# Sparse attention feeding a split-precision feed-forward: four heads to an attention piece, with tiles of the TensorE array

## The chip, the cores and the metric

The kernel runs on one core of one Trainium2 chip. A core has five engines that run their own instruction queues in order: TensorE (PE in the profile, with its weight loads as PEld), VectorE (DVE), ScalarE (ACT), GpSimd (POOL) and SyncE (SP), which issues the DMAs here. Semaphores tie them together. The metric is the device time of one execution in microseconds (us). Before the change it is 994.1 us, the median of three runs (993.43 to 994.18).

## The reference

Eight heads of attention over eight sequences of 576 tokens, head size 64, then a feed-forward layer on the 4608 tokens. Heads 0 to 3 are local (a query sees the 32 keys up to itself), heads 4 to 7 are strided (a query sees the earlier keys at the same place modulo 32).

```
scores = scale * np.matmul(q, k.transpose(0, 1, 3, 2))
rel = pos[:, None] - pos[None, :]
mask_local = (rel >= 0) & (rel < stride)
mask_strided = (rel >= 0) & (pos[None, :] % stride == pos[:, None] % stride)
scores = np.where(masks[None, :, :, :], scores, -1000000000.0)
scores = scores - np.max(scores, axis=-1, keepdims=True)
attn = np.exp(scores)
attn = attn / (np.sum(attn, axis=-1, keepdims=True) + 1e-09)
return np.matmul(attn, v).astype(np.float32)
...
x = np.ascontiguousarray(attn_out.transpose(0, 2, 1, 3)).reshape(B * S, H * D)
...
h = x @ w_in
sp = np.maximum(h, 0.0) + np.log1p(np.exp(-np.abs(h)))
g = h * erf(sp)
return (g @ w_out).astype(np.float32)
```

All operands are float32; w_in is 512 x 2048 and w_out 2048 x 512.

## The kernel before

**Feed-forward.** The tokens go in 12 chunks of 384, the 2048 hidden units in 16 tiles of 128, so there are 192 steps. A step (`ftile`) has 12 matmuls into a PSUM tile h (L457; x and w_in are each split into a high and a low part, three products over four row blocks), a chain of ScalarE and VectorE operations (L465 to L498) that ends in ghi and glo, and 9 matmuls into three PSUM tiles o (L527). These are f32r matmuls of one pass.

**Attention pieces.** Each batch has 12 pieces (`piece`, L220): two heads (a pair hp; 0 and 1 local, 2 and 3 strided) and a third j of the sequence. Local pieces take two blocks of 96 queries, strided ones two blocks of 126 queries or, for j = 2, one of 72. The two heads of a pair lie on the two halves of the 128 rows, and the queries are padded with zeros, so that one matmul (L261) over 128 rows gives 128 keys by the queries of both heads: 192, 252 or 144 columns. These are plain f32 matmuls; the trace shows each as two passes, a weight load and a matmul each. The softmax runs along the key partitions: mask (L282, VectorE, from PSUM into sm), maximum over partitions (L287, GpSimd), subtract (L296, VectorE), exponential (L300, ScalarE). Then come the products with v (L304), one for each head and block, with sm as weights (96, 126 or 72 columns) and 65 moving columns, the last of them ones for the sum; the normalisation (L315, L321, L329); a transpose on TensorE (L335); and the split into xhi and xlo (L353, L358), which the h matmuls read.

The first two batches have a form of their own (mask by a matmul); only the batches from the third on are changed.

**What sets the order.** All operations are added to a planner (`Plan`) with a duration, a key (the time when it is due) and the buffers that it opens and uses. `order` then takes, engine by engine, whichever operation can start first, and by key among those that can start together; the program is written out in that order, and on the chip each engine keeps it. The keys of attention pieces spread them over the feed-forward steps of the two batches before. The PSUM ring `ps` has two tiles; scores, av and transposes take one each. SBUF rings: qk 2, v 3, sm 3, mx 2, xn 2, r 2.

Of the kernel before, what the change touches and what calls it, by code (L numbers as in the profile page):

```python
# [8 lines left out]
F32 = mybir.dt.float32  # L9
# [3 lines left out]
AF = mybir.ActivationFunctionType  # L13
ALU = mybir.AluOpType

B, H, S, D = 8, 8, 576, 64
DM, DF = 512, 2048
NT = B * S
P = 128
# [9 lines left out]
PRO, SLOT = 78.281, 5.385  # L29
# [4 lines left out]
A0K, A0S, A0D = 6.648, 4.179, -9.111  # L34
A1K, A1S, A1D = PRO - 0.655, 3.9, 5.799
ASH, ADT = -0.644, 1.759
# [3 lines left out]
QL = 96  # L40
RB = 7
NA = S // 32
QS = RB * NA
WL = 2 * 2 * QL + 2 * QL + 32
WS = 2 * 2 * QS + 2 * P
# [43 lines left out]
class Plan:  # L89
# [13 lines left out]
    def add(self, eng, dur, key, emit, after=(), new=(), use=(), earliest=0.0):  # L103
        op = Op(eng, dur, key, emit, after, new, use, earliest)
        self.ops.append(op)
        return op

    def _ready(self, op, live):
        t = op.earliest
        for p in op.after:  # L110
            if p.end is None:
                return None
            t = max(t, p.end + (self.SAME if p.eng == op.eng else self.LATENCY)[op.eng])
        for b in op.new:
            order = live.setdefault(b.tag, [])
            n = len(order) - self.bufs[b.tag]
            if n >= 0:
                for u in order[n].users:
                    if u.end is None:
                        return None  # L120
                    t = max(t, u.end + (self.SAME if u.eng == op.eng else self.LATENCY)[op.eng])
        return t
# [46 lines left out]
def attention_moe(  # L169
# [10 lines left out]
    nc = tc.nc  # L180
# [3 lines left out]
    apool = ctx.enter_context(tc.tile_pool(name="apool", bufs=2))  # L184
    mpool = ctx.enter_context(tc.tile_pool(name="mpool", bufs=2))
    wpool = ctx.enter_context(tc.tile_pool(name="wpool", bufs=1))
    ps_a = ctx.enter_context(tc.tile_pool(name="ps_a", bufs=2, space=PSUM))
# [3 lines left out]
    xhi = [cpool.tile([P, RING], F32R, name=f"xhi{c}") for c in range(NCC)]  # L191
    xlo = [cpool.tile([P, RING], F32R, name=f"xlo{c}") for c in range(NCC)]
    ident = cpool.tile([P, P], F32, name="ident")
    con = cpool.tile([P, NCON], BF16, name="con")
    mask_l = con[:, : 2 * QL].rearrange("p (b h q) -> p b h q", b=2, h=1)
    mask_s = con[:, 2 * QL : 2 * QL + QS].rearrange("p (u q) -> p u q", u=1)
# [7 lines left out]
    plan = Plan(bufs)  # L204
    pools = {"apool": apool, "mpool": mpool, "wpool": wpool, "ps_a": ps_a, "ps_h": ps_h, "ps_o": ps_o}

    def buf(pool, tag, shape, name, dtype=F32):
        def make():
            return pools[pool].tile(shape, dtype, tag=tag, name=name, bufs=bufs[tag])

        return Buf(tag, make)

    def dve(n, x=1.0):
        return 0.067 + n * x / 960.0

    def act(n, fixed=0.093):
        return fixed + n / 1200.0


    def piece(b, hp, j, key, dt, ring, pe_mask=False, pool_sub=False, early=False):  # L220
# [4 lines left out]
        loc = hp < 2  # L225
        nblk = 1 if (not loc and j == 2) else 2
        n = QL if loc else (QS if j < 2 else S - 4 * QS)
        units, cols = 2 * nblk, 2 * nblk * n
        pid = f"{b}_{hp}_{j}"
        qk = buf("apool", "qk", [P, WS], f"qk_{pid}")  # L230
        v = buf("apool", "v", [P, 2, 2, D + 1], f"v_{pid}")
        s = buf("ps_h", "h", [P, 512], f"s_{pid}") if early else buf("ps_a", "ps", [P, 512], f"s_{pid}")
        sm = buf("apool", "sm", [P, 4 * QS], f"sm_{pid}")
        mx = buf("apool", "mx", [P, 4 * QS], f"mx_{pid}")
        pav = buf("ps_o", f"o{hp % 2}", [P, 512], f"av_{pid}") if early else buf("ps_a", "ps", [P, 512], f"av_{pid}")
        xn = buf("apool", "xn", [P, 4, D], f"xn_{pid}")
        rc = buf("apool", "r", [P, 4, 1], f"r_{pid}")
        pt = buf("ps_a", "ps", [P, 512], f"t_{pid}")
# [121 lines left out]
        add = plan.add  # L360
        w = nblk * n
        lq = add("sp", P * 4 * (WL if loc else nblk * (2 * n + P)) / 3.6e5, key - 8.0, load_qk, new=[qk])
        lv = add("sp", P * 4 * nblk * 2 * (D + 1) / 3.6e5, key - 7.9, load_v, new=[v])
        per = max(2 * n / 600.0, 0.213) + (2 * n / 2400.0 if pe_mask else 0.0)
        o_s = add("pe", 0.02 + nblk * per, key, scores, [lq, *o_con], [s, sm], [qk])
# [11 lines left out]
        o_e = add("act", act(cols), key + dt + 0.1, exp, [o_b], [], [sm, s] if early else [sm])  # L377
        o_v = add("pe", 0.00174*n * units, key + dt + 0.2, av, [o_e, lv], [pav, xn], [sm, v])
        o_r = add("dve", 0.07, key + 1.5 * dt, total, [o_v], [rc], [pav])
        o_r = add("dve", 0.1, key + 1.5 * dt, invert, [o_r], [], [rc])  # L380
        if early:
            o_n = add("act", 0.2 * units, key + 1.5 * dt + 0.1, norm, [o_r], [], [pav, xn, rc])
        else:
            o_n = add("dve", dve(units * D), key + 1.5 * dt + 0.1, norm, [o_r], [], [pav, xn, rc])
        o_t = add("pe", 0.11 * nblk, key + 2 * dt, transp, [o_n] + ring, [pt], [xn])
        o_h = add("act", act(w, 0.06), key + 2 * dt + 0.1, split_hi, [o_t], [], [pt])
        return [add("dve", dve(w), key + 2 * dt + 0.2, split_lo_x, [o_h], [], [pt])]


    def weight(i, src, rows, sl, key):  # L390
# [175 lines left out]
    o = plan.add("sp", 0.6, -20.0, load_consts, new=[con_f])  # L566
    o_con = [plan.add("dve", 0.6, -19.0, copy_consts, [o], [], [con_f])]
# [3 lines left out]
    x_of = {}  # L571
# [3 lines left out]
    for f in range(0, DF, SW):  # L575
        for c in range(NCC):
            i = len(w1)
            rows, sl = slice(c * P, (c + 1) * P), slice(f, f + SW)
            op, pair = weight(i, w_in, rows, sl, W1K[i // 4] + W1S[i // 4] * (i % 4))
            w1.append(op)  # L580
            win.append(pair)
    for f in range(NFC):
        rows, sl = slice(f * P, (f + 1) * P), slice(0, DM)
        op, pair = weight(NFC + f, w_out, rows, sl, W2K + W2S * f)
# [3 lines left out]
    def order(b):  # L588
        if b % 2:
            return [(hp, j) for j in range(3) for hp in (0, 2, 1, 3)]  # L590
        if b == 0:
            return [(0, 0), (1, 0), (0, 1), (1, 1), (2, 0), (3, 0), (2, 1), (3, 1), (2, 2), (3, 2), (0, 2), (1, 2)]
        return [(hp, j) for j in range(2) for hp in range(2)] + [
            (2, 0), (3, 0), (0, 2), (2, 1), (3, 1), (1, 2), (2, 2), (3, 2)
        ]

    def chunk(c):
        need = [o for b in (2 * (c // 3), 2 * (c // 3) + 1) for o in x_of.get((b, c % 3), [])]
        for f in range(NFC):
            k = c * NFC + f  # L600
            ready = (need + w1[4 * (f // 4) : 4 * (f // 4) + 4], [w2[f]])
            mm1_of[k], _ = ftile(k, ready)
            mm1_first.append(mm1_of[k])

    for b in range(B):
        p2 = b // 2
        for i, (hp, j) in enumerate(order(b)):

            if b % 2 == 0:
                to = [0] if (hp < 2 and j < 2) else ([1] if hp < 2 else [0, 1])  # L610
            else:
                to = [1] if (hp < 2 and j == 0) else ([2] if hp < 2 else [1, 2])
            if b == 0:
                key, dt = A0K + A0S * i, A0D
            elif b == 1:
                key, dt = A1K + A1S * i, A1D
            else:
                if b % 2:
                    slot = 48 * p2 - 3 + (15 * i) / 11
                elif i < 4:  # L620
                    slot = 48 * (p2 - 1) + 13 + 4 * i
                else:
                    slot = 48 * (p2 - 1) + 29 + (15 * (i - 4)) / 7
                key, dt = PRO + SLOT * (slot + ASH), ADT * SLOT
            ring = []
            if p2:
                ring = [mm1_of[48 * (p2 - 1) + 16 * c + 15] for c in to]
            done = piece(b, hp, j, key, dt, ring, pe_mask=b < 2, pool_sub=False, early=b == 0)
            for c in to:
                x_of.setdefault((b, c), []).extend(done)  # L630
        if b % 2 == 0:
            continue
        for c in range(3 * p2, 3 * p2 + 3):
            chunk(c)
# [109 lines left out]
```

## Time and profile before

| what | us |
| --- | --- |
| median of three runs | 994.1 |
| profiled execution, its own time | 993.13 |
| its span, first to last instruction | 991.2 |
| third batch's attention to the last piece, about | 118 to 816 |
| score products L261, whole span: union of busy time, 192 / 252 / 144 columns | 43.1 / 33.6 / 6.7 |
| products with v L304, whole span: 96 / 126 / 72 columns | 39.3 / 32.0 / 6.6 |

The union counts a matmul from its start to its modelled end, and neighbours overlap, so these times are longer than what a group takes from the engine. The chain of work that ended last gives that: at each step it goes back to what released an instruction, or to the instruction before it on its engine, and the pieces of the chain add up to the span.

### The profile page before, as it was taken

The numbers are of one execution on the slowest core, as the hardware profiler recorded it, in microseconds if no ns is written. First come the engines' busy times: TensorE is split into PE (matmuls) and PEld (weight loads), VectorE is DVE, ScalarE is ACT, GpSimd is POOL, SyncE is SP. The second block draws the span as 40 slices with busy tenths as digits, with TensorE's granted clock in tenths as the row PEclk, the third lists the DMA queues.
The fourth block names the chain that finished last, engine by engine and source line by source line (L and its number), as shares of the span: only waits on it lengthen the run. The fifth ranks groups of instructions, "written<-read, shape, count | busy, mean of one in ns | idle before, by whom it ended". The sixth has DMA issues, their size and how long they took to land.

```text
span 991.2 us, 15250 instructions
## 1 busy us (share of the span) xinstructions
PE 979.5 (99%) x5443; PEld 885.6 (89%) x5443; DVE 728.7 (74%) x1619; ACT 654.7 (66%) x1481; POOL 152.8 (15%) x100
## 2 busy tenths in 40 slices
PE   8999999999999999999999999999999999999998
PEld 6788999999899989999899999999899999999997
DVE  6999997677677776676777776776767776665664
ACT  4676777567566666666765665766766576766765
POOL 3534111111112110011112110111111210000000
PEclk9999999999999999999999999999999999999999
DMA  9994211111222211111222220211112220000000
GB/s 310 308 338 144 63 35 59 40 40 53 71 62 82 62 37 38 46 53 27 80 58 73 71 63 19 70 40 40 49 53 66 63 63 1 32 2 0 32 1 33
DMA packets 37659, 68.76 MB, mean 69 GB/s; under 512 B 4176, under 2 KB 18640, under 8 KB 37584
## 3 DMA queue, kind: packets, MB, share of 16 engines
q1 hardware_dynamic: 37584, 67.80, 22.1%
q8 instruction: 43, 0.70, 0.3%
q14 instruction: 32, 0.26, 0.1%
HBM read 58.34 MB, written 9.44 MB: 68 GB/s over the span
## 4 chain that ended last, share of the span: by engine, by line
PE 91%; DVE 8%; ACT 0%; issue 0%; DMA 0%
PE h L457 39%; PE o L527 39%; PE s L261 5%; PE av L304 5%; DVE w L415 1%; PE t L335 1%; DVE w L421 1%; DVE pair L429 1%; DVE a L462 1%; DVE w L408 1%; DVE glo L498 1%; DVE b L492 0%; DVE xlo L358 0%; DVE b L462 0%; PE warm L638 0%
## 5 line engine op out<-in xcount | busy, mean ns | idle before, releaser
L527 PE MATMUL o<-pair,ghi 128*128 128x512 f32 x1152 | 372.3, 404 | 0.0
L457 PE MATMUL h<-xhi,pair 128*128 128x384 f32 x1536 | 306.7, 341 | 1.4 <-DVE b L492 1.4
L457 PEld LDWEIGHTS h<-xhi,pair 128*128 128x128 f32 x1536 | 271.9, 188 | 15.7 <-DVE b L492 3.8
L465 ACT ACTIVATE b<-b 128x384 f32<-128x384 f32 x384 | 199.7, 521 | 104.2 <-DVE b L462 101.6
L287 POOL PARTITION_ALL_REDUCE mx<-sm x96 | 152.6, 1594 | 664.1 <-DVE sm L282 568.7
L527 PEld LDWEIGHTS o<-pair,ghi 128*128 128x128 f32 x1152 | 207.0, 188 | 28.0
L527 PE MATMUL o<-pair,glo 128*128 128x512 f32 x576 | 225.9, 392 | 0.0
L457 PE MATMUL h<-xlo,pair 128*128 128x384 f32 x768 | 165.9, 337 | 0.0
L498 DVE TENSOR_TENSOR glo<-b,ghi 128x384 fp32r<-128x384 f32 x192 | 110.5, 576 | 60.3 <-ACT ghi L495 59.8
L462 DVE SCALAR_TENSOR_TENSOR a<-h,a 128x384 f32<-128x384 f32 x192 | 106.4, 554 | 64.9 <-ACT a L465 63.3
L457 PEld LDWEIGHTS h<-xlo,pair 128*128 128x128 f32 x768 | 137.2, 187 | 0.0
L462 DVE SCALAR_TENSOR_TENSOR a<-a,h 128x384 f32<-128x384 f32 x192 | 105.5, 549 | 40.7 <-ACT b L465 38.6
L465 ACT ACTIVATE b<-a 128x384 f32<-128x384 f32 x192 | 100.5, 524 | 47.6 <-DVE glo L498 47.1
L527 PEld LDWEIGHTS o<-pair,glo 128*128 128x128 f32 x576 | 108.1, 188 | 24.1
L495 ACT CAST ghi<-b 128x384 fp32r<-128x384 f32 x192 | 97.9, 510 | 46.8 <-PE o L527 41.6
L492 DVE TENSOR_TENSOR b<-b,h 128x384 f32<-128x384 f32 x192 | 105.1, 547 | 31.2 <-ACT b L465 30.9
L465 ACT ACTIVATE a<-a 128x384 f32<-128x384 f32 x192 | 100.2, 522 | 26.6 <-DVE a L462 24.3
L465 ACT ACTIVATE a<-h 128x384 f32<-128x384 f32 x192 | 92.7, 483 | 33.4 <-PE h L457 32.3
L462 DVE SCALAR_TENSOR_TENSOR b<-b,a 128x384 f32<-128x384 f32 x192 | 110.5, 576 | 3.2
L304 PEld LDWEIGHTS av<-v,sm 128*96 128x96 f32 (+2 forms) x704 | 78.0, 171 | 7.8 <-ACT sm L300 1.5
L261 PE MATMUL s<-qk 128*128 128x192 f32 (+2 forms) x352 | 83.4, 351 | 0.1
L304 PE MATMUL av<-v,sm 128*96 128x65 f32 (+2 forms) x704 | 77.9, 251 | 1.1 <-ACT sm L279 0.7
(34 smaller groups left out, 588.4 us busy)
## 6 DMA issues: line engine op xcount, KB each, us to landing
qk<-qk_loc SPq DMA_DIRECT2D x48, 304.0 KB, 2.8
qk<-qk_str SPq DMA_DIRECT2D x32, 380.0 KB, 3.2
v<-v_all SPq DMA_DIRECT2D x80, 130.0 KB, 2.1
out<-ob SPq DMA_DIRECT2D x36, 256.0 KB, 2.1
words<-w_in SPq DMA_DIRECT2D x16, 512.0 KB, 5.6
words<-w_out SPq DMA_DIRECT2D x16, 512.0 KB, 5.9
qk<-qk_str SPq DMA_DIRECT2D x16, 136.0 KB, 2.1
v<-v_all SPq DMA_DIRECT2D x16, 65.0 KB, 1.9
```

Source lines behind the costliest of these rows:

```text
L261: yield nc.tensor.matmul(dst, qk[:, k0 + blk * step : k0 + blk * step + P], qk[:, blk * 2 * n : (blk + 1) * 2 * n], start=blk == 0, stop=n ...
L287: yield nc.gpsimd.partition_all_reduce(mx[:, :cols], sm[:, :cols], P, ReduceOp.max)
L304: yield nc.tensor.matmul(pav[:n, u * (D + 1) : (u + 1) * (D + 1)], sm[:, u * n : (u + 1) * n], v[:, u // 2, u % 2, :], start=True, stop=True,)
L335: yield nc.tensor.transpose(pt[:, blk * n : (blk + 1) * n], xn[:n, 2 * blk : 2 * blk + 2, :].rearrange("p h d -> p (h d)"), ident[:n, :n],)
L408: yield nc.vector.tensor_scalar(out=w.tile.bitcast(U32), in0=words[:, :, 1], scalar1=0x07FFFFFF, scalar2=3, op0=ALU.bitwise_and, op1=ALU.l ...
L457: yield nc.tensor.matmul(ph[:, :CH], win[4 * s + cc][:, w, fs], x[cc][:, c0 : c0 + CH], start=(i == 0), stop=(i == len(terms) - 1))
L462: yield nc.vector.scalar_tensor_tensor(out=out, in0=in0, scalar=scalar, in1=in1, op0=op0, op1=op1)
L465: yield nc.scalar.activation(dst, src, func, bias=bias[i], scale=scale)
L492: yield nc.vector.tensor_tensor(out=bb.tile, in0=bb.tile, in1=ph[:, :CH], op=ALU.mult)
L495: yield nc.scalar.copy(ghi.tile, bb.tile)
L498: yield nc.vector.tensor_tensor(out=glo.tile, in0=bb.tile, in1=ghi.tile.bitcast(F32), op=ALU.subtract)
L527: yield nc.tensor.matmul(po.tile, g[:, ts], wout[f][:, w], start=(f == 0 and i == 0), stop=(f == NFC - 1 and i == 2),)
```

## The change

From the third batch on, two pairs of heads that are of one kind (0 and 1, or 2 and 3) make one piece, `quad`, in place of two. A batch has 6 of them in place of 12. The parts:

- Scores: for two-block quads, 8 matmuls (L452 of the new kernel), each on the 64 rows of one head, 128 keys by 96 or 126 queries, in one go. The two heads of a pair write different PSUM banks, in turn. The zero padding is no longer read. The short strided quads keep matmuls over 128 rows.
- Mask, maximum, subtract and exponential run once for each bank, that is twice for a two-block quad and once for a short one.
- Products with v: 16 matmuls (L499), each former one parted at query 64, into partitions 0 to 63 and from 64 on, which are two column tiles of the array.
- Normalisation twice, transposes of both pairs into one PSUM tile, split twice.
- The keys: the even batches' quads are 8 and 4 steps apart, the odd batches' 3. The planner's check for free buffers now counts buffers of one ring that one operation opens together. Ring sizes stay.

```diff
-        for b in op.new:
+        for i, b in enumerate(op.new):
             order = live.setdefault(b.tag, [])
-            n = len(order) - self.bufs[b.tag]
+            n = len(order) - self.bufs[b.tag] + sum(x.tag == b.tag for x in op.new[:i])
...
+    def quad(b, loc, j, key, dt, ring):
...
+        hps = (0, 1) if loc else (2, 3)
+        nblk = 1 if (not loc and j == 2) else 2
+        n = QL if loc else (QS if j < 2 else S - 4 * QS)
+        units, w = 2 * nblk, nblk * n
+        tiled = nblk == 2
+        nbank = 2 if nblk == 2 else 1
+        cols = 4 * w // nbank
...
+        s = [buf("ps_a", "ps", [P, 512], f"s{i}_{pid}") for i in range(nbank)]
+        pav = [buf("ps_a", "ps", [P, 512], f"av{i}_{pid}") for i in range(2)]
...
+        def place(i, blk, h):
+
+            if tiled:
+                return h, (2 * i + blk) * n
...
+        def scores():
+            k0, step = units * n, n if loc else P
+            used = set()
+            for i in range(2):
+                for blk in range(nblk):
+                    keys = slice(k0 + blk * step, k0 + blk * step + P)
+                    for h in range(2) if tiled else (slice(0, 2),):
+                        rows = slice(h * D, (h + 1) * D) if tiled else slice(0, P)
+                        bank, c = place(i, blk, h if tiled else 0)
+                        q0 = (blk * 2 + (h if tiled else 0)) * n
+                        width = n if tiled else 2 * n
+                        yield nc.tensor.matmul(
+                            s[bank][:, c : c + width], qk[i][rows, keys], qk[i][rows, q0 : q0 + width],
+                            start=bank not in used,
+                            stop=True, skip_group_check=True,
+                        )
+                        used.add(bank)
...
+        def av():
+            for i in range(2):
+                for u in range(units):
+                    bank, c = place(i, u // 2, u % 2)
+                    for lo, hi in ((0, 64), (64, n)) if tiled else ((0, n),):
+                        yield nc.tensor.matmul(
+                            pav[i][lo:hi, u * (D + 1) : (u + 1) * (D + 1)],
+                            sm[bank][:, c + lo : c + hi],
+                            v[i][:, u // 2, u % 2, :],
+                            start=True,
+                            stop=True,
+                        )
...
+        for k in range(nbank):
+            o = add("dve", dve(cols), key + 0.1 + 0.01 * k, mask(k), [o_s], [], [s[k], sm[k]])
+            o = add("pool", 0.4 + cols * 0.0028, key + 0.2 + 0.01 * k, maxi(k), [o], [mx[k]], [sm[k]], earliest=6.7)
+            o = add("dve", dve(cols), key + dt + 0.01 * k, sub(k), [o], [], [mx[k], sm[k]])
+            o_e.append(add("act", act(cols), key + dt + 0.1 + 0.01 * k, exp(k), [o], [], [sm[k]]))
...
+            for i, (loc, j) in enumerate(pairs(b)):
+                to = chunks_of(b, loc, j)
+                slot = 48 * p2 - 3 + 3 * i if b % 2 else 48 * (p2 - 1) + (13 + 8 * i if i < 2 else 29 + 4 * (i - 2))
```

**Where the instructions move.** All places are the seventh batch, j = 1, local heads. In the names, s is a score tile, av a product with v, t a transpose; a former piece is named by its pair and j (0_1 and 1_1), a quad by batch, kind and j (6_0_1), and the last number only tells buffers apart. The first place is TensorE's row of scores. Before, pair 0 and, some 70 rows later, pair 1 in the same way:

```order
L335 MATMUL t_1_0_6835<-ident,xn_1_0_6763 128x96 x2
L261 MATMUL s_0_1_6840<-qk_0_1_6511 128x192 x2
L527 MATMUL o_6_6178<-pair_1786,ghi_6738 128x512 x2
L527 MATMUL o_6_6178<-pair_1786,glo_6754 128x512
L527 MATMUL o_6_6189<-pair_1786,ghi_6738 128x512 x2
```

Now, both pairs:

```order
L648 MATMUL h_7046<-xlo_83,pair_289 128x384
L452 MATMUL s_6_0_1_7066<-qk_6_0_1_6706 128x96
L452 MATMUL s_6_0_1_7067<-qk_6_0_1_6706 128x96
L452 MATMUL s_6_0_1_7066<-qk_6_0_1_6706 128x96
L452 MATMUL s_6_0_1_7067<-qk_6_0_1_6706 128x96
L452 MATMUL s_6_0_1_7066<-qk_6_0_1_6723 128x96
L452 MATMUL s_6_0_1_7067<-qk_6_0_1_6723 128x96
L452 MATMUL s_6_0_1_7066<-qk_6_0_1_6723 128x96
L452 MATMUL s_6_0_1_7067<-qk_6_0_1_6723 128x96
L718 MATMUL o_6_6336<-pair_1802,ghi_6955 128x512 x2
```

Four matmuls of 192 columns in two places have become eight of 96 in one, in turn into two PSUM tiles. The second place is TensorE's products with v. Before, pair 0 alone:

```order
L457 MATMUL h_6918<-xlo_82,pair_517 128x384
L457 MATMUL h_6918<-xlo_83,pair_483 128x384
L304 MATMUL av_0_1_6941<-v_0_1_6532,sm_0_1_6841 96x65 x4
L457 MATMUL h_6950<-xhi_76,pair_590 128x384
L457 MATMUL h_6950<-xhi_77,pair_558 128x384
```

Now the first eight of sixteen (the other eight, with av_6_0_1_7147, follow at once):

```order
L718 MATMUL o_6_6336<-pair_1940,glo_7062 128x512
L499 MATMUL av_6_0_1_7146<-v_6_0_1_6759,sm_6_0_1_7068 64x65
L499 MATMUL av_6_0_1_7146<-v_6_0_1_6759,sm_6_0_1_7068 32x65
L499 MATMUL av_6_0_1_7146<-v_6_0_1_6759,sm_6_0_1_7069 64x65
L499 MATMUL av_6_0_1_7146<-v_6_0_1_6759,sm_6_0_1_7069 32x65
L499 MATMUL av_6_0_1_7146<-v_6_0_1_6759,sm_6_0_1_7068 64x65
L499 MATMUL av_6_0_1_7146<-v_6_0_1_6759,sm_6_0_1_7068 32x65
L499 MATMUL av_6_0_1_7146<-v_6_0_1_6759,sm_6_0_1_7069 64x65
L499 MATMUL av_6_0_1_7146<-v_6_0_1_6759,sm_6_0_1_7069 32x65
```

Each matmul of 96 queries has become two, of 64 and of 32, and the burst reads both halves of the softmax (7068 and 7069). The third place is VectorE's softmax rows. Before:

```order
L282 TENSOR_TENSOR sm_0_1_6841<-s_0_1_6840,con 128x384
L462 SCALAR_TENSOR_TENSOR a_6858<-h_6799,a_6858 128x384
L492 TENSOR_TENSOR b_6832<-b_6832,h_6741 128x384
L462 SCALAR_TENSOR_TENSOR a_6812<-a_6812,h_6780 128x384
L462 SCALAR_TENSOR_TENSOR b_6866<-b_6866,a_6812 128x384
L498 TENSOR_TENSOR glo_6892<-b_6832,ghi_6876 128x384
L296 TENSOR_TENSOR sm_0_1_6841<-sm_0_1_6841,mx_0_1_6869 128x384
```

Now:

```order
L468 TENSOR_TENSOR sm_6_0_1_7068<-s_6_0_1_7066,con 128x384
L468 TENSOR_TENSOR sm_6_0_1_7069<-s_6_0_1_7067,con 128x384
L653 SCALAR_TENSOR_TENSOR a_7087<-h_7046,a_7087 128x384
L683 TENSOR_TENSOR b_7064<-b_7064,h_6989 128x384
L689 TENSOR_TENSOR glo_7124<-b_7009,ghi_7107 128x384
L483 TENSOR_TENSOR sm_6_0_1_7068<-sm_6_0_1_7068,mx_6_0_1_7097 128x384
L483 TENSOR_TENSOR sm_6_0_1_7069<-sm_6_0_1_7069,mx_6_0_1_7109 128x384
```

Masks and subtracts stand two in a row, with three feed-forward operations between them in place of five. Between the quad's scores and its products with v, TensorE has 12 h and 21 o matmuls.

More of the change, by code (lines that the diff above doesn't have):

```diff
@@ L211, in buf, with named @@
         return Buf(tag, make)
+    def named(name, f):
+        f.__name__ = name
+        return f
     def dve(n, x=1.0):
@@ L387, in piece, with load_qk, load, load_v @@
         return [add("dve", dve(w), key + 2 * dt + 0.2, split_lo_x, [o_h], [], [pt])]
+    def quad(b, loc, j, key, dt, ring):
[6 more added lines that the diff above has]
+        cols = 4 * w // nbank
+        pid = f"{b}_{hps[0]}_{j}"
+        qk = [buf("apool", "qk", [P, WS], f"qk{i}_{pid}") for i in range(2)]
+        v = [buf("apool", "v", [P, 2, 2, D + 1], f"v{i}_{pid}") for i in range(2)]
+        s = [buf("ps_a", "ps", [P, 512], f"s{i}_{pid}") for i in range(nbank)]
+        sm = [buf("apool", "sm", [P, 4 * QS], f"sm{i}_{pid}") for i in range(nbank)]
+        mx = [buf("apool", "mx", [P, 4 * QS], f"mx{i}_{pid}") for i in range(nbank)]
+        pav = [buf("ps_a", "ps", [P, 512], f"av{i}_{pid}") for i in range(2)]
+        xn = [buf("apool", "xn", [P, 4, D], f"xn{i}_{pid}") for i in range(2)]
+        rc = [buf("apool", "r", [P, 4, 1], f"r{i}_{pid}") for i in range(2)]
+        pt = buf("ps_a", "ps", [P, 512], f"t_{pid}")
+        def place(i, blk, h):
+            if tiled:
+                return h, (2 * i + blk) * n
+            c = (blk * 2 + h) * n
+            return (i, c) if nbank == 2 else (0, i * 2 * w + c)
+        def load_qk(i):
+            def load():
+                if loc:
+                    yield nc.sync.dma_start(qk[i][:, :WL], qk_loc[b, hps[i], j])
+                else:
+                    cw = nblk * (2 * n + P)
+                    yield nc.sync.dma_start(qk[i][:, :cw], qk_str[b, hps[i] - 2, j, :, :cw])
+            return load
+        def load_v(i):
+            def load():
+                cw = nblk * 2 * (D + 1)
+                yield nc.sync.dma_start(
+                    v[i].tile.rearrange("p b h d -> p (b h d)")[:, :cw], v_all[b, hps[i], j, :, :cw]
+                )
+            return load
+        def scores():
[15 more added lines that the diff above has]
+                        used.add(bank)
+        def mask(k):
+            def run():
+                src, dst = s[k][:, :cols], sm[k][:, :cols]
+                if loc:
+                    m = (mask_l if j == 0 else mask_l[:, 1:2]).rearrange("p b h q -> p h b q")
+                    r, z, m = "p (i b q) -> p i b q", dict(i=2, b=2), m.broadcast_to([P, 2, 2, n])
+                else:
+                    r, z = "p (u q) -> p u q", dict(u=cols // n)
+                    m = mask_s[:, :, :n].broadcast_to([P, cols // n, n])
+                yield nc.vector.tensor_tensor(
+                    out=dst.rearrange(r, **z), in0=src.rearrange(r, **z), in1=m, op=ALU.add
+                )
+            return named("mask", run)
+        def maxi(k):
+            def run():
+                yield nc.gpsimd.partition_all_reduce(mx[k][:, :cols], sm[k][:, :cols], P, ReduceOp.max)
+            return named("maxi", run)
+        def sub(k):
+            def run():
+                d = sm[k][:, :cols]
+                yield nc.vector.tensor_tensor(out=d, in0=d, in1=mx[k][:, :cols], op=ALU.subtract)
+            return named("sub", run)
+        def exp(k):
+            def run():
+                d = sm[k][:, :cols]
+                yield nc.scalar.activation(d, d, AF.Exp, scale=1.0 / D**0.5)
+            return named("exp", run)
+        def av():
[9 more added lines that the diff above has]
+                            stop=True,
+                        )
+        def norm(i):
+            a, rr = lambda: pav[i][:n, : units * (D + 1)].rearrange("p (u d) -> p u d", u=units), lambda: rc[i][:n, :units]
+            def total():
+                yield nc.vector.tensor_scalar(
+                    out=rr(), in0=a()[:, :, D : D + 1], scalar1=1e-9, scalar2=None, op0=ALU.add
+                )
+            def invert():
+                yield nc.vector.reciprocal(rr(), rr())
+            def scale():
+                yield nc.vector.tensor_tensor(
+                    out=xn[i][:n, :units], in0=a()[:, :, :D], in1=rr().broadcast_to([n, units, D]), op=ALU.mult
+                )
+            return total, invert, scale
+        def transp():
+            for i in range(2):
+                for blk in range(nblk):
+                    c = i * w + blk * n
+                    yield nc.tensor.transpose(
+                        pt[:, c : c + n], xn[i][:n, 2 * blk : 2 * blk + 2, :].rearrange("p h d -> p (h d)"), ident[:n, :n]
+                    )
+        def views(i, t):
+            base, src = (b % 2) * S, pt[:, i * w : (i + 1) * w]
+            if loc:
+                c0 = base + j * 2 * QL
+                return src, t[:, c0 : c0 + w]
+            r0 = 2 * RB * j
+            dst = t[:, base : base + S].rearrange("p (a r) -> p a r", r=32)[:, :, r0 : r0 + w // NA]
+            return src.rearrange("p (r a) -> p a r", a=NA), dst
+        def split(i):
+            def split_hi():
+                src, hi = views(i, xhi[hps[i]])
+                yield nc.scalar.copy(hi, src)
+            def split_lo_x():
+                src, hi = views(i, xhi[hps[i]].bitcast(F32))
+                _, lo = views(i, xlo[hps[i]])
+                yield nc.vector.tensor_tensor(out=lo, in0=src, in1=hi, op=ALU.subtract)
+            return split_hi, split_lo_x
+        add = plan.add
+        lq = [add("sp", P * 4 * (WL if loc else nblk * (2 * n + P)) / 3.6e5, key - 8.0 + 0.1 * i, load_qk(i), new=[qk[i]]) for i in range(2)]
+        lv = [add("sp", P * 4 * nblk * 2 * (D + 1) / 3.6e5, key - 7.8 + 0.1 * i, load_v(i), new=[v[i]]) for i in range(2)]
+        d_s = 1.27 if tiled else 2 * nblk * max(2 * n / 600.0, 0.213)
+        o_s = add("pe", d_s, key, scores, [*lq, *o_con], [*s, *sm], [*qk])
+        o_e = []
+        for k in range(nbank):
[3 more added lines that the diff above has]
+            o_e.append(add("act", act(cols), key + dt + 0.1 + 0.01 * k, exp(k), [o], [], [sm[k]]))
+        o_v = add("pe", 1.23 if tiled else 0.00174 * n * 2 * units + 0.05, key + dt + 0.2, av, [*o_e, *lv], [*pav, *xn], [*sm, *v])
+        o_n = []
+        for i in range(2):
+            total, invert, scale = norm(i)
+            o = add("dve", 0.07, key + 1.5 * dt, total, [o_v], [rc[i]], [pav[i]])
+            o = add("dve", 0.1, key + 1.5 * dt, invert, [o], [], [rc[i]])
+            o_n.append(add("dve", dve(units * D), key + 1.5 * dt + 0.1, scale, [o], [], [pav[i], rc[i], xn[i]]))
+        o_t = add("pe", 0.09 + 0.11 * 2 * nblk, key + 2 * dt, transp, o_n + ring, [pt], [*xn])
+        done = []
+        for i in range(2):
+            hi, lo = split(i)
+            o = add("act", act(w, 0.06), key + 2 * dt + 0.1, hi, [o_t], [], [pt])
+            done.append(add("dve", dve(w), key + 2 * dt + 0.2, lo, [o], [], [pt]))
+        return done
@@ L603, in chunk, with pairs, chunks_of @@
             mm1_first.append(mm1_of[k])
+    def pairs(b):
+        if b % 2:
+            return [(True, 0), (False, 0), (True, 1), (False, 1), (True, 2), (False, 2)]
+        return [(True, 0), (True, 1), (False, 0), (True, 2), (False, 1), (False, 2)]
+    def chunks_of(b, loc, j):
+        if b % 2 == 0:
+            return [0] if (loc and j < 2) else ([1] if loc else [0, 1])
+        return [1] if (loc and j == 0) else ([2] if loc else [1, 2])
     for b in range(B):
         p2 = b // 2
[L607 to L626, printed above, removed]
+        if p2 == 0:
+            for i, (hp, j) in enumerate(order(b)):
+                to = chunks_of(b, hp < 2, j)
+                key, dt = (A0K + A0S * i, A0D) if b == 0 else (A1K + A1S * i, A1D)
+                done = piece(b, hp, j, key, dt, [], pe_mask=True, pool_sub=False, early=b == 0)
+                for c in to:
+                    x_of.setdefault((b, c), []).extend(done)
+        else:
+            for i, (loc, j) in enumerate(pairs(b)):
+                to = chunks_of(b, loc, j)
+                slot = 48 * p2 - 3 + 3 * i if b % 2 else 48 * (p2 - 1) + (13 + 8 * i if i < 2 else 29 + 4 * (i - 2))
                 ring = [mm1_of[48 * (p2 - 1) + 16 * c + 15] for c in to]
-            done = piece(b, hp, j, key, dt, ring, pe_mask=b < 2, pool_sub=False, early=b == 0)
-            for c in to:
-                x_of.setdefault((b, c), []).extend(done)
+                done = quad(b, loc, j, PRO + SLOT * (slot + ASH), ADT * SLOT, ring)
+                for c in to:
+                    x_of.setdefault((b, c), []).extend(done)
         if b % 2 == 0:
```

## The prediction

> **What bounds the kernel now.** I read the share of each engine first, then the chain of work that ended last, then the waits of TensorE in the stretch the change touches. That stretch runs from about 118 us, where the attention of the third batch begins, to 816 us, where the last attention piece is done.
>
> ```profile
> span 991.2 us, 15250 instructions
> PE 979.5 (99%) x5443; PEld 885.6 (89%) x5443; DVE 728.7 (74%) x1619; ACT 654.7 (66%) x1481; POOL 152.8 (15%) x100
> PE 91%; DVE 8%; ACT 0%; issue 0%; DMA 0%
> 118.00:816.00 698.00, 697.33 (x3866) 636.80 (x3865) 512.75 (x1153) 459.49 (x1024) 105.23 (x71) 1.00 0.19 54
> PEld h L457 <- DVE b L492: 2.8, 6, 0.7
> by line: PE h L457 42.0%; PE o L527 40.6%; PE av L304 6.5%; PE s L261 6.5%; PE t L335 1.7%; DVE glo L498 0.7%; DVE a L462 0.6%; DVE b L492 0.4%; DVE sm L282 0.4%; ACT b L465 0.2%; DVE b L462 0.2%; DVE xn L329 0.1%; DVE r L321 0.1%; issue 0.
> ```
>
> The fourth row is the stretch: its length, then the busy time of PE, PEld, DVE, ACT and POOL. PE is busy 697.33 of 698.00 us at a granted clock of 1.00, and the only wait of its weight loads that the stretch shows is 2.8 us. VectorE is busy 512.75 us (73%), ScalarE 66%. So here a microsecond less on TensorE is a microsecond less in the time, as long as no new wait takes its place. The last row is the chain within the stretch: score products (s) and products with v (av) take 6.5% each, 45 us each of 698. This is all the change can win on.
>
> **What one piece costs.** The chain also gives the time by which each group of matmuls pushes PE on, which is what I need; the mean durations of single matmuls overlap and would count twice. From the chain in order of time (start, length, what):
>
> ```profile
> 398.41 2.05 PE o L527 x9
> 400.46 0.17 PE t L335 x2
> 400.62 0.68 PE s L261 x4
> ...
> 406.85 2.12 PE h L457 x12
> ...
> 450.31 0.22 PE t L335 x2
> 450.53 0.65 PE av L304 x8
> ...
> 452.63 0.85 PE s L261 x4
> ...
> 459.22 0.83 PE av L304 x8
> ...
> 473.90 0.65 PE s L261 x4
> ...
> 483.12 0.65 PE av L304 x8
> 483.77 2.18 PE h L457 x12
> 485.95 0.24 PE s L261 x2
> ...
> 492.62 0.25 PE av L304 x4
> L304 PE MATMUL av<-v,sm x516: 217/248/273, 132.1 to 812.7; 128*96 128x65 f32 x93, 128*126 128x65 f32 x64, 128*72 128x65 f32 x15
> L261 PEld LDWEIGHTS s<-qk 128*128 128x128 f32 x352 | 60.7, 193 | 9.0 <-issue 1.9 <-DMA qk<-qk_loc 0.6
> ```
>
> Scores: 0.65 us for a local piece (two f32 matmuls, each in two passes, so four entries, 192 columns moving), 0.85 us for a strided one (252 moving), 0.24 us for a short one (144). Per pass that is 0.162, 0.212 and 0.12 us: 0.84 ns for each moving column. Products with v: 0.65 us in eight passes at 96 weight columns, 0.83 us at 126, 0.25 us in four at 72. Per pass 0.081, 0.104 and 0.062 us, which follows the weight columns at 0.84 ns each, though only 65 columns move (those alone would take 0.055). So a pass costs 0.84 ns times the larger of its weight columns and its moving columns. Behind a product with v the next twelve h matmuls take 2.18 in place of 2.12 us, so I add 0.06 us to each: 0.71 and 0.89.
>
> Batches three to eight have 6 x 6 = 36 local pieces, 24 long strided ones and 12 short ones. The change takes the first 60 pairwise into 30 tiled bursts. Before, these cost 36 x 0.65 + 24 x 0.85 = 43.8 us for scores and 36 x 0.71 + 24 x 0.89 = 46.9 us for av, 90.7 us together. The short ones keep their matmuls (two pieces side by side, no tiles) and the transposes are as many as before; I count both as unchanged. Their 0.24, 0.25 and 0.22 us only stand closer together.
>
> **What a tiled burst costs.** No instruction of before uses part of the array, so I bound it. A score burst is 8 matmuls on 64 rows, 16 passes, each with 128 weight columns and 96 or 126 moving: by the rule above 128 x 0.84 = 0.108 us a pass, whichever piece it is. If the two row halves work side by side, 8 x 0.108 = 0.86 us; if one after the other, 1.73. An av burst is 16 matmuls, 32 passes, with at most 64 weight columns and 65 moving, 0.055 us a pass: 16 x 0.055 = 0.88 us side by side, 1.76 in turn. I take side by side for both, since the halves share neither rows nor PSUM bank in the scores, and neither columns nor partitions in av.
>
> Then there is the change of shape, once into and once out of each burst. It lies between nothing and a full drain with a bare weight load behind it. A 65-column matmul ends no sooner than 217 ns after it starts, 55 of which are its stream, so a drain is some 0.16 us; a 128-column weight load takes 193 ns (last row). I take 0.19 us, the load beginning while the array drains, between the ends 0 and 0.35. It is the value nearest to a row, the 193 ns. So a score burst is 0.86 + 0.38 = 1.24, an av burst 0.88 + 0.38 = 1.26: 1.25 us each, 60 x 1.25 = 75.0 us. Gain: 90.7 - 75.0 = **15.7 us**.
>
> Here a page of the Trainium skill bears on the sum. "TensorEngine Tiling (Array Packing)", section Key Properties, says that changing the tiling mode drains TensorE, not merely changing the tile. No row of before shows it; by it the end at 0 (956 us, the first rival) falls away, and the 979 us below stay.
>
> **New waits.** The av burst now waits for both halves of the softmax. I follow the local quad of the seventh batch whose order stands in the part on the change: between its scores and its av stand 21 o matmuls and 12 h matmuls.
>
> ```profile
> 638.03 0.84 PE L261 MATMUL s<-qk 128*128 128x192 f32 x4
> 640.57 0.55 DVE L282 TENSOR_TENSOR sm<-s,con 128x384 f32<-128x384 f32 x1
> 641.28 1.58 POOL L287 PARTITION_ALL_REDUCE mx<-sm  x1 [18.10 <-DVE sm L282]
> 644.30 0.55 DVE L296 TENSOR_TENSOR sm<-sm,mx 128x384 f32<-128x384 f32 x1
> 644.89 0.53 ACT L300 ACTIVATE sm<-sm 128x384 f32<-128x384 f32 x1
> 647.06 0.81 PE L304 MATMUL av<-v,sm 128*96 128x65 f32 x8
> PE h L457 <- DVE b L492: 0.7, 3, 0.2
> ```
>
> At 2.12 us for twelve h and 2.05 / 9 = 0.228 us for an o, PE has 2.12 + 21 x 0.228 = 6.9 us of other work there. The chain: mask 0.55, 0.16 to POOL (641.28 - 641.12), two reductions of 1.58 one behind the other, subtract 0.55, exponential 0.53: 5.0 us, the second mask lying under the first reduction. That leaves 1.9 us for queueing on VectorE and ScalarE. The piece in the rows lost 1.7 us ahead of its mask (its scores end at 638.87) and 1.4 us ahead of its subtract (641.28 + 1.58 = 642.86), and had 1.6 us to spare before av. In the quad the second kind of loss lies mostly under the second reduction: the new order has three MoE operations, 3 x 0.55 us, between masks and subtracts, some 2.8 us with the masks, while the reductions end after 3.9. The first kind fits in the 1.9 us, just. So most bursts find their input ready and some do not: I take 1.5 us over all 36, say six stalls of a quarter microsecond; the ends are 0 and 36 x 0.4 = 14 us. Behind a stalled av in PE's queue stand o and h matmuls, so a stall is lost in full; so far h waits 0.7 us in the stretch (last row). VectorE and ScalarE keep their work (two masks in a row in place of two apart), so the 73% becomes 75% of a shorter stretch.
>
> A quad takes both qk buffers, so the loads of the next quad go out only after its scores. The two score bursts nearest to each other (the last ones of the fourth batch) have 24 h and 3 o matmuls between them, 2 x 2.12 + 3 x 0.228 = 4.9 us; a load takes 2.1 to 3.2 us to land. I cost it at nothing; without that cover PE would wait some 3 us for each of 36 bursts, and it would be plain as a wait for DMA.
>
> ```profile
> qk<-qk_loc SPq DMA_DIRECT2D x48, 304.0 KB, 2.8
> qk<-qk_str SPq DMA_DIRECT2D x32, 380.0 KB, 3.2
> qk<-qk_str SPq DMA_DIRECT2D x16, 136.0 KB, 2.1
> ```
>
> Sum: -15.7 + 1.5 = -14.2 us. The profiled execution took 993.1 us, 1.9 above its span of 991.2 and 1 below the median of 994.1: 993.1 - 14.2 = **979 us**.
>
> **The rivals.**
> - *Cheap changes of shape.* At 0 instead of 0.38 us a burst: 60 x 0.38 = 22.8 us less, 956 us. For it: weight loads lie beside matmuls nearly always (PEld 89% beside PE 99%), so a load may be hidden across a change too. Against it: a drain of 0.16 us would have to be hidden as well. 0.10.
> - *Dear changes of shape.* At 0.35 each, 0.70 a burst: 60 x 0.32 = 19 us more, 998 us, slower than before. It decides from 0.31 us a change on. 0.07.
> - *The column tiles of av take turns* (slower). Weight loads of one tile can't lie under the other's matmul, so 32 passes come one by one: 0.88 us more in 30 bursts, 26 us, 1005 us. It turns the sign once more than half of the overlap is lost (14.2 / 30 = 0.47 us). For it: both tiles use the same 128 rows. Against it: in the rows below eight weight loads of av lie beside its eight matmuls, on the same rows. 0.12.
>
> ```profile
> 409.26 0.90 PEld L304 LDWEIGHTS av<-v,sm 128*96 128x96 f32 x8
> 409.49 0.81 PE L304 MATMUL av<-v,sm 128*96 128x65 f32 x8
> ```
>
>   The Trainium skill has a rule that gives this outcome: "TensorE: Matmul & The Clock Gate", Part 3 (Packing small matmuls), says that a weight load overlaps running matmuls only where the row group differs. By the two rows that does not hold for the whole array; for column tiles no run here shows it.
> - *The row tiles take turns,* or the parts are no tiles at all, so that the change doesn't do what it says: 0.87 us more in 30 bursts, 26 us, 1005 us; with the one before, 1031 us. 0.06.
> - *The softmax of two pieces comes late:* 14 us of stalls, 979 + 12.5 = 991 us, no change to a little faster. For it: the second reduction. Against: the spare above. 0.08.
>
> **How the numbers follow.** The forecast has 0.57; its own range is 970 to 987 us. The range for 8 in 10 runs from the cheap changes to the dear ones, 956 to 999 us, and leaves out tiles that take turns (0.18). About 2 us (0.2%) is what a measurement of this kernel can tell from no change. Faster: 0.57 + 0.10 + half of the late softmax = 0.71. Same: the rest of it and a part of the dear changes, 0.07. Slower: 0.22.
>
> **What would show it.** In the chain, a burst of 16 score passes and one of 32 av passes should each take about 1.25 us, alike for local and strided quads; s and av should fall from 45 us each in the stretch to about 40. If av bursts take over 2 us, the column tiles take turns; if only the first passes behind a burst stretch, it is the changes. Idle time of PE ahead of av, released by ScalarE's exponential, would be the late softmax. The forecast is wrong if PE stays at 99% and the time does not fall, for then a tiled pass costs more than its columns.

## The result, and the profile after

The changed kernel takes 1027.9 us (median of four runs, 1027.6 to 1028.93) against 994.1 us before: a ratio of 1.0338, 95% interval 1.032 to 1.0356. It is slower by 3.4%, where 979 us and at most 999 had been forecast. The profiled execution has a span of 1025.8 us, 34.6 more than before.

The rows that answer to those of before, from the page, the waits of PE's weight loads and the chain in the stretch from 118 to 850 us (the last attention piece now ends near 850):

```profile
span 1025.8 us, 16728 instructions
PE 1013.7 (99%) x6163; PEld 883.2 (86%) x6163; DVE 722.8 (70%) x1607; ACT 654.1 (64%) x1475; POOL 147.6 (14%) x94
PEld h L648 <- DVE b L683: 1.0, 4, 0.3
PEld av L499 <- ACT sm L490: 0.7, 2, 0.4
by line: PE h L648 41.4%; PE o L718 40.6%; PE av L499 11.8%; PE s L452 4.7%; PE t L529 1.6%
```

PE is still busy 99% of the time, and the h matmuls wait less than before (1.0 us against 2.8). The products with v waited 0.7 us in all for the exponential. So no new wait took the place of the gain: it is PE's own bursts that take longer. The chain says which. Scores fell from 6.5% of 698 us, 45 us, to 4.7% of 732, 34 us. Products with v rose from 45 us to 11.8%, 86 us.

The chain in order of time shows that the rise is in the local bursts alone, 18 of the 30:

```profile
562.03 3.92 PE av L499 x32
568.90 1.09 PE s L452 x16
...
743.61 1.08 PE av L499 x31
744.69 2.28 PE h L648 x12
...
767.59 1.07 PE s L452 x16
768.66 2.28 PE h L648 x12
770.94 4.80 PE o L718 x21
775.73 3.92 PE av L499 x32
```

Score bursts take 1.07 us local and 1.09 strided. Products with v take 1.08 us in a strided quad (one record of 32 is missing at 743.61) and 3.92 in a local one, for the same 32 passes. The chain puts the end of a burst on the group behind it (2.28 us for twelve h in place of 2.12). Measured from the start of the last matmul ahead of a burst to the start of the second one behind it, less two ordinary steps from matmul to matmul (0.176 us after an h, 0.227 after an o), the means are 1.27 and 1.29 us for scores, 1.28 for strided and **4.12 for local products with v**. The forecast had 1.25 for all of them.

One difference between the two kinds is the width of the second column tile: 126 queries are parted into 64 and 62, 96 queries into 64 and 32. The weight loads, each shape apart (busy, mean ns, then idle time of the queue just before them), over the same stretch:

```profile
L499 PEld LDWEIGHTS av<-v,sm 128*64 128x64 f32 x480 | 39.6, 135 | 21.0 <-issue 3.8 <-ACT b L656 3.0 <-ACT ghi L686 1.1
L499 PEld LDWEIGHTS av<-v,sm 128*32 128x32 f32 x288 | 19.8, 108 | 9.8
L499 PEld LDWEIGHTS av<-v,sm 128*62 128x62 f32 x192 | 11.9, 135 | 0.0
```

Ahead of the loads of 62 columns there is no idle time at all. Ahead of those of 32 there are 9.8 us, with no releaser named: the profile shows nothing that was waited for in these pauses. Ahead of those of 64, which open every burst and also follow each tile of 32, there are 21.0 us.

### The profile page after: what moved, and what is told of

It reads as the page before. It is cut to its first block, busy times and chain, and to the rows that moved or that the text cites. A ratio compares the mean times of both kernels' runs of the same rounds, so it can differ in the third digit from the quotient of the medians.

```text
span 1025.8 us, 16728 instructions
## 1 busy us (share of the span) xinstructions
PE 1013.7 (99%) x6163; PEld 883.2 (86%) x6163; DVE 722.8 (70%) x1607; ACT 654.1 (64%) x1475; POOL 147.6 (14%) x94
## 4 chain that ended last, share of the span: by engine, by line
PE 92%; DVE 6%; DMA 1%; issue 0%; ACT 0%; SPq 0%
PE o L718 39%; PE h L648 39%; PE av L499 8%; PE s L452 3%; DVE w L606 1%; DVE w L612 1%; PE t L529 1%; DVE pair L620 1%; DVE w L599 1%; PE s L265 1%; DMA words<-w_in 1%; PE av L308 0%; DVE xlo L362 0%; DMA qk<-qk_loc 0%; DVE a L653 0%; DVE b L653 0%
## 5 line engine op out<-in xcount | busy, mean ns | idle before, releaser
L718 PE MATMUL o<-pair,ghi 128*128 128x512 f32 x1152 | 364.3, 397 | 0.0
L476 POOL PARTITION_ALL_REDUCE mx<-sm x66 | 101.5, 1577 | 641.9 <-DVE sm L468 641.9
L499 PEld LDWEIGHTS av<-v,sm 128*64 128x64 f32 (+2 forms) x1008 | 63.4, 128 | 31.3 <-issue 3.8
L499 PE MATMUL av<-v,sm 128*64 128x65 f32 (+2 forms) x1008 | 89.6, 233 | 0.0
L291 POOL PARTITION_ALL_REDUCE mx<-sm x24 | 45.9, 1929 | 63.9 <-ACT sm L283 58.2
```

The costliest lines, as they stand in the source:

```text
L291: yield nc.gpsimd.partition_all_reduce(mx[:, :cols], sm[:, :cols], P, ReduceOp.max)
L476: yield nc.gpsimd.partition_all_reduce(mx[k][:, :cols], sm[k][:, :cols], P, ReduceOp.max)
L499: yield nc.tensor.matmul(pav[i][lo:hi, u * (D + 1) : (u + 1) * (D + 1)], sm[bank][:, c + lo : c + hi], v[i][:, u // 2, u % 2, :], start=Tr ...
L718: yield nc.tensor.matmul(po.tile, g[:, ts], wout[f][:, w], start=(f == 0 and i == 0), stop=(f == NFC - 1 and i == 2),)
```

## The experiments

The theory that these rows suggest: a tile of 32 columns is another shape of the array than a tile of 64, so each step between them drains the array (a pass of the new shape has to wait until those under way are through). A local burst steps 15 times inside, a strided one never. If 32 passes of 0.055 us come in turn and the way in and out costs 0.38, then 15 x = 4.12 - 1.76 - 0.38 and a step costs 0.13 us. The rivals: that tiles cost as much in any widths, that local pieces are slow for another reason, and that a tile of 32 is slow in itself. All kernels keep the planner's durations and keys of the changed kernel.

**Local products with v whole.**

```diff
-                    for lo, hi in ((0, 64), (64, n)) if tiled else ((0, n),):
+                    for lo, hi in ((0, 64), (64, n)) if tiled and not loc else ((0, n),):
```

> The products with v of the local quads go back to whole matmuls of 96 weight columns, the strided ones keep their two column tiles of 64 and 62. In the profile of the changed kernel a strided av burst took 1.28 us and a local one (tiles of 64 and 32) 4.12 us. Theory 1 (a column tile of 32 after one of 64 is another shape of the array, and each change of shape drains it, 0.13 us each, 15 times inside a local burst): a local burst becomes 16 passes of 0.085 us, 1.4 us, 18 bursts save 18 x 2.7 = 49 us, 979 us, 1.5% faster than before. Theory 2 (tiled av costs whatever its widths, and the strided bursts only look cheap because their cost is recorded elsewhere): the saving is less than half of that, the time stays above 1003 us.

It took 978.8 us, ratio to before 0.9851 (0.9828 to 0.9874). All of the loss, and a gain of 1.5%, hang on the local products. The strided ones keep their tiles and their 1.28 us.

**Both local tiles 64 wide.** The second tile reads 32 columns of no use; those behind the last block are set to zero.

```diff
-                    for lo, hi in ((0, 64), (64, n)) if tiled else ((0, n),):
+                    for lo, hi in ((0, 64), (64, P if loc else n)) if tiled else ((0, n),):
...
+                if loc:
+                    yield nc.vector.memset(sm[k][:, cols : cols + 32], 0.0)
```

> Local quads: the second column tile is widened from 32 to 64 weight columns (32 columns of no use behind the queries, zeros behind the last ones, by a memset of 32 columns on VectorE), so both tiles have one shape; the output is unchanged. Theory 1 (unequal widths change the shape): a local burst falls from 4.12 to the strided 1.28 us, 18 x 2.84 = 51 us, 977 us. Theory 3 (local bursts are slow for another reason, such as the layout of the local softmax tile): no change, 1028 us.

It took 976.3 us, ratio 0.982 (0.9803 to 0.9836): with more weight columns, 51.6 us faster than the change. A local burst in its chain, and the weight loads of the products with v from 118 to 815 us:

```profile
677.96 1.08 PE av L501 x32
...
L501 PEld LDWEIGHTS av<-v,sm 128*64 128x64 f32 x768 | 30.4, 137 | 9.2 <-issue 3.8 <-ACT b L658 3.0 <-ACT ghi L688 1.1
L501 PEld LDWEIGHTS av<-v,sm 128*62 128x62 f32 x192 | 11.9, 135 | 0.0
```

The burst is 1.08 us, as a strided one, and the idle time ahead of weight loads is down from 30.8 us (21.0 + 9.8) to 9.2. Of what is left, the 3.8, 3.0 and 1.1 us at the row's end stood there before too: they are the first loads of the 30 bursts.

The starts of the single passes show where the time went. In the changed kernel (the burst at 656.34 us) two passes of 64 columns and two of 32 follow each other, and the starts lie 0.108, 0.152, 0.081 and 0.150 us apart, 0.49 us for each four, over and over: no two passes go side by side. In this run (the burst at 677.89 us) the passes of the two tiles start 0.007 us apart, and such a pair follows the one before after about 0.058 us.

**Three tiles of 32.**

```diff
-                    for lo, hi in ((0, 64), (64, n)) if tiled else ((0, n),):
+                    for lo, hi in ((0, 32), (32, 64), (64, 96)) if loc else ((0, 64), (64, n)) if tiled else ((0, n),):
```

> Local quads: the 96 queries are parted into three column tiles of 32, all of one shape, 24 matmuls a burst. Theory 1: no change of shape inside the burst; if three tiles work side by side, 16 x 0.055 + 0.38 = 1.3 us a burst and 977 us; if tiles of this shape take turns, 48 x 0.055 + 0.38 = 3.0 us and 1008 us. Theory 4 (a 32-wide tile is itself slow, 0.27 us more for each of its matmuls): 24 such matmuls in place of 8, each burst 4.3 us longer, 1105 us.

It took 977.2 us, ratio 0.9828 (0.9809 to 0.9846). A tile of 32 is not slow, and three of one shape work side by side as two do:

```profile
621.30 1.05 PE av L499 x48
```

48 passes in 1.05 us.

**The same widths, grouped.** The two loops are exchanged for local quads, so that four matmuls of 64 columns come in a row and then four of 32.

```diff
-                for u in range(units):
-                    bank, c = place(i, u // 2, u % 2)
-                    for lo, hi in ((0, 64), (64, n)) if tiled else ((0, n),):
+                parts = ((0, 64), (64, n)) if tiled else ((0, n),)
+                both = [(u, p) for p in parts for u in range(units)] if loc else [(u, p) for u in range(units) for p in parts]
+                for u, (lo, hi) in both:
+                    bank, c = place(i, u // 2, u % 2)
+                    if True:
```

> Local quads: the same 16 matmuls of 64 and 32 columns, but four of 64 in a row and then four of 32, so 3 changes of shape inside a burst in place of 15; neighbours now use the same tile and take turns. Theory 1: 32 x 0.055 + 3 x 0.13 + 0.38 = 2.5 us in place of 4.12, 18 x 1.6 = 28 us less, 1000 us. Theory 4 (a 32-wide tile is itself slow): no change, 1028 us.

One run took 999.5 us. The burst is 2.38 us in the chain, 2.58 measured as above: the same matmuls, 12 changes of shape fewer, 1.55 us less, 0.13 us a change.

```profile
636.09 2.38 PE av L501 x32
```

This run also parts the two losses of the mixed burst. Of 4.12 us, 15 changes make 2.0; that the passes of a mixed or grouped burst come in turn makes 0.9, since with 3 changes (0.4 us) a burst still takes 2.58 in place of 1.28. In its trace passes of one width start 0.055 to 0.061 us apart, one by one.

**The fault put into the strided quads.** The kernel with equal local tiles, the strided second tile parted again.

```diff
-                    for lo, hi in ((0, 64), (64, P if loc else n)) if tiled else ((0, n),):
+                    for lo, hi in ((0, 64), (64, P)) if loc else ((0, 64), (64, 96), (96, n)) if tiled else ((0, n),):
```

> As the kernel with equal tiles of 64 and 64 in the local quads (976.3 us), but now the strided quads get unequal ones: the second column tile of 62 is parted into 32 and 30, so each block has a tile of 64 and two of 32. Theory 1 (a change of width changes the shape and drains the array, 0.13 us each): 15 changes inside a strided burst, 8 x (0.11 + 0.11) + 15 x 0.13 + 0.38 = 4.1 us in place of 1.28, 12 x 2.8 = 34 us, 1010 us. Theory 3 (something in the local pieces themselves was slow): strided bursts stay near 1.3 us, 976 us.

One run took 1010.9 us, 34.6 more than with equal tiles. The strided burst (48 passes) now has the local one's time, and the local one (32) the strided one's:

```profile
642.27 1.08 PE av L501 x32
668.23 1.09 PE s L452 x16
677.85 3.96 PE av L501 x48
```

Measured with its ends the strided burst takes 4.16 us, where 4.1 had been expected from 15 changes. So it follows the widths and not the pieces.

**What each part of the change is worth.** Three more runs take away the tiles one by one, and one goes further with them. All products with v whole:

```diff
-                    for lo, hi in ((0, 64), (64, n)) if tiled else ((0, n),):
+                    for lo, hi in ((0, n),):
```

> As the kernel with whole local products with v (978.8 us), but the strided ones are whole too, 16 passes at 126 weight columns; scores keep their 64-row tiles. If a strided burst of two equal tiles is really cheaper by the difference of its prices (1.28 us against 2 x 0.89 = 1.78), the time goes up by 12 x 0.5 = 6 us, 985 us. If tiles of equal width only pay for their changes of shape, no difference, 979 us.

984.0 us, ratio 0.9899 (0.9882 to 0.9915): 5.1 us above the run with only the local ones whole, 6 expected. Two column tiles of equal shape do gain on strided quads.

Scores over 128 rows, equal tiles of v kept; the local mask follows the new places (block by head in place of head by block):

```diff
-            if tiled:
-                return h, (2 * i + blk) * n
...
-                    for h in range(2) if tiled else (slice(0, 2),):
-                        rows = slice(h * D, (h + 1) * D) if tiled else slice(0, P)
-                        bank, c = place(i, blk, h if tiled else 0)
-                        q0 = (blk * 2 + (h if tiled else 0)) * n
-                        width = n if tiled else 2 * n
+                    for h in (0,):
+                        rows = slice(0, P)
+                        bank, c = place(i, blk, 0)
+                        q0 = blk * 2 * n
+                        width = 2 * n
```

> As the kernel with equal tiles of 64 and 64 (976.3 us), but the scores of a quad are 4 matmuls over all 128 rows with zero-padded queries, as before the change, in one go. By the prices of before (0.65 and 0.85 us a piece) against the measured tiled bursts (1.27 and 1.29): local 18 x 0.03, strided 12 x 0.41, together 5.5 us more, 982 us. If 64-row tiles gained on local quads too, as side-by-side passes without the changes would (0.9 us), the loss is over 12 us, 988 us.

982.5 us, ratio 0.9886 (0.9871 to 0.9901): 6.2 us above, 5.5 expected. In its chain a whole local score burst takes 1.30 us and a strided one 1.70:

```profile
649.66 1.70 PE s L450 x8
...
673.94 1.30 PE s L450 x8
```

Against 1.27 and 1.29 us tiled, nearly all of it is the strided quads: on local ones the two changes of shape eat the gain.

Both edits at once, quads without tiles:

> Quads with no tiles at all: whole scores and whole products with v, four heads to a piece. It prices the regrouping alone. If the two gains above add up: 978.8 + 6 + 5.5 = 990 us, 4 us faster than before, from fewer bursts between the feed-forward matmuls. If the regrouping is neutral as my prediction had it: 994 us. If its longer softmax chain costs waits: over 996 us.

990.3 us, ratio 0.9963 (0.995 to 0.9976), as the sum of the gains had it. The regrouping alone is 4 us faster than before; the forecast had counted it as 1.5 us slower. The span is 2.9 us shorter. The weight loads of h wait 0.6 us in the stretch from 118 to 816, where they waited 2.8 before:

```profile
PEld h L646 <- DVE b L681: 0.6, 2, 0.3
```

Fewer bursts give some 1.2 us more: from 110 us on, all bursts with scores, av and transposes (neighbours taken as one, measured as above) are 168 before and cost 111.3 us, now 110 that cost 110.1. The two together cover the 2.9. Why VectorE hands over b in better time was not tried apart.

Scores in four tiles of 64 rows by 64 keys, with the equal tiles of v:

```diff
-                    keys = slice(k0 + blk * step, k0 + blk * step + P)
-                    for h in range(2) if tiled else (slice(0, 2),):
+                    for h, half in ((0, 0), (1, 0), (0, 1), (1, 1)) if tiled else ((slice(0, 2), 0),):
+                        kw = 64 if tiled else P
+                        keys = slice(k0 + blk * step + 64 * half, k0 + blk * step + 64 * half + kw)
...
-                            s[bank][:, c : c + width], qk[i][rows, keys], qk[i][rows, q0 : q0 + width],
-                            start=bank not in used,
+                            s[bank][64 * half : 64 * half + kw, c : c + width], qk[i][rows, keys], qk[i][rows, q0 : q0 + width],
+                            start=(bank, half) not in used,
```

> As the kernel with equal tiles of 64 and 64 (976.3 us), but each score matmul of 128 keys is parted into two column tiles of 64 keys, so four tiles of 64 x 64 work side by side. A pass is then bound by its moving columns (0.081 and 0.106 us) and no longer by 128 weight columns (0.112). If four tiles overlap as two do: a burst costs 8 x 0.081 + 0.38 = 1.03 us local and 1.23 strided, 18 x 0.24 + 12 x 0.06 = 5 us less, 971 us. If twice as many instructions cost more than that, 976 us or above.

972.3 us, ratio 0.9783 (0.9768 to 0.9798). It is the fastest kernel of this study, 2.2% faster than before and 5.4% faster than the change (972.3 / 1027.9). Its score bursts in the chain, local and strided:

```profile
641.52 1.02 PE s L453 x32
...
665.32 0.82 PE s L453 x32
```

The rows are of a strided and a local quad in that order; with the ends the means are 1.22 and 1.02 us, against 1.29 and 1.27 with two tiles.

## Why the prediction was wrong

Point by point, by its own steps.

- *TensorE is the bound, and a microsecond of it is one of the time.* Right, in both directions: the sum of the measured bursts is 18 x (4.12 - 1.42) = 48.6 us more for local products, 12 x 0.5 = 6.0 less for strided ones, 18 x 0.03 + 12 x 0.41 = 5.5 less for scores, together 37 us more; the waits of PE fell by some 2 us, and the span grew by 34.6.
- *A pass costs 0.84 ns times the larger of its weight and moving columns, and tiles work side by side.* Right for row tiles (burst forecast 1.24 us, measured 1.27 and 1.29) and for column tiles of one shape (forecast 1.26, measured 1.28).
- *A change of shape costs 0.19 us.* Right in size for the way into and out of a burst: in 1.27 us of scores 16 passes side by side are 0.86, which leaves 0.2 us each. The reason given for it, a weight load of 193 ns that begins while the array drains, no run shows, and a change between tiles of 64 and 32 columns has another price, 0.13 us.
- *The step that failed* stands in the part on what a tiled burst costs: "an av burst is 16 matmuls, 32 passes, with at most 64 weight columns", side by side for both kinds, and the change of shape "once into and once out of each burst". That 96 parted at 64 leaves 32, a tile of another shape, was written in the rows of the order (64x65 and 32x65 in turn) and was not put to the rule that is priced there. In 18 of 30 bursts there are 15 more changes inside. At the 0.19 us of the prediction itself they come to 15 x 0.19 = 2.85 us a burst and 18 x 2.85 = 51 us. The runs show as much in all (4.12 - 1.28 = 2.84), but as 2.0 us of changes at 0.13 and 0.9 of passes that come in turn, so that the two sums agree is chance. The Trainium skill's "TensorEngine Tiling (Array Packing)", section Key Properties, cited there, says just this: a change of mode drains TensorE, a change of tile does not. The runs agree on the cost: 12 changes fewer save 1.55 us, and none inside leaves 1.28 us. They show a pause at each change; that it is a drain they do not show by itself.
- *The rivals.* That column tiles take turns gave 1005 us, and both kinds of tiles in turn 1031, close to the measured 1027.9. That number came near by chance: column tiles as such do not take turns, since the strided bursts overlap and so do the local ones in equal tiles, and the row tiles overlap too (1.27 us). Only in the bursts of two widths do the passes come in turn, for 0.9 of the 2.84 us. The rule that the first leaned on, in the Trainium skill's "TensorE: Matmul & The Clock Gate", Part 3, by which a weight load overlaps running matmuls only where the row group differs, does not hold here: the column tiles share all rows, and 32 passes took 1.08 us in the chain. The cheap and the dear changes (0 and 0.35 us) are both excluded by the 0.13 to 0.2 us measured.
- *New waits, 1.5 us, or 14 us with a late softmax.* Wrong in sign and small: the run without tiles shows the regrouping to be a gain of 4 us, and in the changed kernel av waited 0.7 us for the exponential.
- *The signs by which it was to be judged.* That bursts should be "alike for local and strided quads" did its work: it failed at once, and pointed at the widths. The other one, that av bursts of over 2 us mean column tiles that take turns, would have misled: the local bursts fit it, and only 0.9 us of them is turns. So would the last, by which a time that does not fall at 99% PE means tiled passes dearer than their columns: in tiles of one shape they cost what their columns cost (1.28 us against 1.26).

With equal widths the change takes 976.3 us, where the prediction had 979. Of these 18 us of gain the tiles give 14 (990.3 to 976.3) and the regrouping 4, where the prediction had 15.7 and a loss of 1.5; the 979 came near because these two errors partly cancel.

## What to carry to other kernels

Count changes of the array's shape matmul by matmul, not burst by burst: a remainder that is much narrower than its neighbour (32 beside 64 here, not 62) is another shape, and where it alternates with its neighbour the tiles stop overlapping as well. Pad the odd part to the width of its neighbour, or take a divisor of the length for all tiles; either turned a loss of 34 us into a gain of 17 to 18 here. Where a cost has been priced, look for it in each row of the new order before it is multiplied by a count.

## What the runs showed of the hardware

- A tile of 62 columns behaves as one of 64 (no idle time ahead of its weight loads, bursts of 1.28 us), a tile of 32 does not, so the shape goes by steps of width and not by the exact count. A tile of 30 likewise goes as one of 32 (4.16 us in the run whose strided quads had 64, 32 and 30, as 15 changes would have it), and the whole-array products of 72, 96 and 126 columns before the change show no such cost (0.062, 0.081 and 0.104 us a pass, 0.84 ns a column). Widths between 32 and 62 were not tried.
- A change between tiles of 64 and 32 columns cost 0.13 us (15 in 4.12 us, 12 fewer for 1.55 us); the way between the whole array and tiles about 0.2 us.
- Three column tiles of 32 took 1.25 us for 48 passes and two of 64 took 1.28 for 32: a third overlapping tile cost nothing here.
